# Attention ahead of two expert layers: the first query block's keys in one chunk, a batch's logit products ahead of its transposes, and the value products of two block pairs in one run

## The chip, the cores and the metric

The kernel runs on one core of a Trainium2 chip. The number that counts is the device time of one execution in microseconds (us): 776.23 us is the median of three runs of the kernel before, 775.80 to 778.62. Five engines work side by side, each through its own instructions in the order of the program: TensorE (PE, matrix products and transposes), VectorE (DVE), ScalarE (ACT), GpSimd (POOL) and SyncE (SP, which here issues most of the DMA transfers). They wait for each other through semaphores. PE writes into PSUM, which is cut into eight banks; ACT and DVE copy from there into SBUF.

## The reference, cut to what matters

Three layers follow each other: attention over 4 batches of 8 heads, 768 positions and 64 channels per head, with a local window of 96 keys and 8 global keys, and then two layers of 8 experts over the 3072 tokens. The change is in the attention alone, and in the products with the gates that are interleaved with it:

```python
scores = scale * np.matmul(q, k.transpose(0, 1, 3, 2))
keep = is_global | is_local          # 8 first keys, and the 96 latest up to the query
scores = np.where(keep, scores + bias, -1000000000.0)
scores = scores - np.max(scores, axis=-1, keepdims=True)
a = np.exp(scores)
a = a / (np.sum(a, axis=-1, keepdims=True) + 1e-09)
out = np.matmul(a, v)
...
skip_score = x @ w_skip              # x: the 8 heads' outputs side by side, 512 wide
logits = xc @ w_gate                 # first expert layer
logits = x @ w_gate                  # second expert layer
```

## The kernel before, in words

**Tiling.** A head pair (two heads of one batch, 16 pairs in all) is worked on in six query blocks i of 128 positions. Block 0 sees its own 128 keys. Each other block sees `KW` = 232 keys: 96 before it, its own 128 and the 8 global ones. For the value products the keys stand on partitions, so 232 keys are cut into two chunks r of 116 (keys two by two, even and odd), and block 0's 128 keys, in the same way, into two of 64. `VW` holds the values of blocks 1 to 5, `V0` those of block 0; `load_v` fetches both.

**Units.** Two query blocks (x = 0, 1) of a head pair are a unit, numbered g; there are 48, and j = 0, 1, 2 is a unit's place in its head pair. Block 0 is x = 0 of the unit with j = 0. The stages of a unit are:

- `qk_t`: PE transposes the raw q and k of two blocks into a PSUM tile `pP`, DVE copies the k half into `KT`, POOL copies the keys that the next blocks share, ACT copies the q half into `QT`;
- `s_stage`: PE makes the scores (`pS`, two banks, one unit's worth), DVE adds the bias and takes the extreme of each row (`sb`, `st`);
- `e_stage`: ACT takes the exponentials (`pb`) and their sums;
- `n_stage`: DVE makes the reciprocals of the sums, POOL multiplies `pb` with them, four instructions;
- `t_stage`: PE transposes `pb` of one block into a `pP` tile, DVE copies it to `pts`;
- `o_stage`: PE multiplies `pts` with the values into the one bank `pO`, ACT copies the result to `XT`.

**The order of the work.** One Python loop over g writes all of it, and each engine keeps this order. In its iteration g stand `e_stage(g+2)`, `o_stage(g-1)`, up to two entries of the list `todo`, `n_stage(g+1)`, `t_stage(g)` for both blocks, one part of `qk_t` and `s_stage(g+3)`. I name an iteration by the j of its unit g-1: J0, J1 and J2 follow each other and make up a head pair. On PE an iteration is thus: value products, `todo`, eight transposes of `pb`, four of k and q, four score products (each fp32 product shows as two matmul records in the trace).

**The list `todo`.** When XT has 384 finished positions of a head pair, `x_stage` is put on it (PE transposes them, three in a run, ACT copies to `xs`, SP writes to the tables `xd` and `x2d`). With the last head pair of a batch `logits` (products of XT with the three gates, copied by ACT to `ls`) and `logits_t` (PE transposes `ls`, DVE sums up into `LG`) come behind it. After the last unit what is left of `todo` is worked off, with the steps `ww` (products of the second layer's weights) between, and `route1` sorts the tokens, one batch at a time, on DVE.

**PSUM.** `pP` has five banks that are used in turn by `qk_t`, `t_stage`, `x_stage` and `logits`; `pS` has two, `pO` one.

The lines that write the order of one iteration (before):

```python
        ex(0, 0)
        ex(0, 1)
        if g >= 1:
            o_stage(g - 1)
        if g >= 0:
            one_task()
            if len(todo) > 1:
                one_task()
        if 0 <= g + 1 < NU:
            n_stage(g + 1)
        ex(1, 0)
        if 0 <= g < NU:
            t_stage(g, 0)
            t_stage(g, 1)
        ex(1, 1)
```

Of the kernel before, what the change touches and what calls it, by code (L numbers as in the profile page):

```python
# [7 lines left out]
F32 = mybir.dt.float32  # L8
# [4 lines left out]
AF = mybir.ActivationFunctionType  # L13
# [157 lines left out]
def tile_attn_moe_moe(ctx: ExitStack, tc: tile.TileContext, q, k, v, n_global, n_local,  # L171
                      w_skip, w_gate, w1, w2, w2_gate, w21, w22, out):
    nc = Chip(tc.nc)
    global CK
    CK = ck = nc.clock
    B, H, S, D = q.shape
    G, W = int(n_global), int(n_local)
    HP = H // 2
# [26 lines left out]
    ident = consts.tile([128, 128], F32, name="ident")  # L205
# [42 lines left out]
    ld = att.enter_context(tc.tile_pool(name="ld", bufs=2))  # L248
    wk = att.enter_context(tc.tile_pool(name="wk", bufs=2))
    ps = att.enter_context(tc.tile_pool(name="ps", bufs=1, space=bass.MemoryType.PSUM))  # L250
# [12 lines left out]
    VW, V0 = {}, {}  # L263

    def load_v(b, hp):
        w = VW[b, hp] = ld.tile([KP, NI - 1, 2, 2, D], F32, name="vw", bufs=3)
        z = V0[b, hp] = ld.tile([64, 2, 2, D], F32, name="v0", bufs=3)
        vv = v[b, 2 * hp:2 * hp + 2].rearrange("h (i x) d -> h i x d", x=128)
        nc.sync.dma_start(z.rearrange("p h r d -> p h (r d)"),
                          vv[:, 0].rearrange("h (p r) d -> p h (r d)", r=2))  # L270
        for h in range(2):
            def part(p0, p1, src):
                nc.sync.dma_start(w[p0:p1, :, h].rearrange("p i r d -> p i (r d)"),
                                  src.rearrange("i (p r) d -> p i (r d)", r=2))
            part(W // 2, KP - G // 2, vv[h, 1:])
            part(0, W // 2, vv[h, :NI - 1, 128 - W:])
            part(KP - G // 2, KP, vv[h, 0:1, :G].to_broadcast([NI - 1, G, D]))
# [36 lines left out]
    KT, QT, XT, PB, PT, ST, pO, LS = {}, {}, {}, {}, {}, {}, {}, {}  # L314
# [24 lines left out]


    NG = NI // 2
    GR = [(b, hp, j) for b in range(B) for hp in range(HP) for j in range(NG)]
    SB = {}

    def keys(i):
        return KW if i else 128

    def s_stage(g):
# [11 lines left out]
        for x in range(2):  # L360
            i = 2 * j + x
            SB[g, x] = sb = wk.tile([128, 2, KW], F32, name="sb", bufs=4)
            for h in range(2):
                nc.vector.tensor_tensor_reduce(sb[:, h, :keys(i)], p_s[i, h][:, :keys(i)],
                                               (bias1 if i else bias0)[:, 2 * hp + h, :], 1.0, 3e38,
                                               op0=OP.add, op1=OP.min, accum_out=st[:, 0, x, h:h + 1])

    def e_stage(g, x, h):
        n = keys(2 * GR[g][2] + x)
        if h == 0:  # L370
            PB[g, x] = wk.tile([128, 2, 2, KP], F32, name="pb", bufs=6)
        nc.scalar.activation(PB[g, x][:, h, :, :n // 2].rearrange("p r k -> p k r"),
                             SB[g, x][:, h, :n].rearrange("p (k r) -> p k r", r=2), AF.Exp,
                             bias=ST[g][:, 0, x, h:h + 1], scale=-1.0, accum_out=ST[g][:, 1, x, h:h + 1])
        if h == 1:
            SB.pop((g, x))

    def n_stage(g):
        st = ST.pop(g)
        nc.vector.tensor_scalar(st[:, 2], st[:, 1], 1e-9, None, op0=OP.add)  # L380
        nc.vector.reciprocal(st[:, 2], st[:, 2])
        for x in range(2):
            n = keys(2 * GR[g][2] + x)
            for h in range(2):
                p = PB[g, x][:, h, :, :n // 2]
                nc.gpsimd.tensor_scalar(p, p, st[:, 2, x, h:h + 1], 1.0, op0=OP.mult, op1=OP.mult)

    def t_stage(g, x):
        n = keys(2 * GR[g][2] + x) // 2
        pt = ps.tile([128, 2, 2, 128], F32, name="pP", bufs=5)  # L390
        p = PB.pop((g, x))
        for h in range(2):
            for r in range(2):
                nc.tensor.transpose(pt[:n, h, r, :], p[:, h, r, :n], ident)
        PT[g, x] = wk.tile([128, 2, 2, 128], F32, name="pts", bufs=3)
        nc.vector.tensor_copy(PT[g, x][:n], pt[:n])

    def o_stage(g):
        b, hp, j = GR[g]
        po = ps.tile([128, 2, 128], F32, name="pO")  # L400
        for x in range(2):
            i = 2 * j + x
            n = keys(i) // 2
            t = PT.pop((g, x))
            for r in range(2):
                for h in (1, 0):
                    vv = VW[b, hp][:, i - 1, h, r, :] if i else V0[b, hp][:, h, r, :]
                    nc.tensor.matmul(po[h * 64:(h + 1) * 64, x, :], vv, t[:n, h, r, :], start=r == 0, stop=r == 1)
        if b not in XT:
            XT[b] = wk.tile([128, HP, S], F32, name="xT")  # L410
        nc.scalar.activation(XT[b][:, hp, j * 256:(j + 1) * 256], po.rearrange("p a b -> p (a b)"), AF.Copy)

    def x_stage(b, hp, g):
        px = ps.tile([128, 3, 128], F32, name="pP", bufs=5)
# [407 lines left out]
    todo = [(late_consts, ())]  # L822
# [35 lines left out]
    for g in range(-3, NU + 1):  # L858
        ex = (lambda x, h: e_stage(g + 2, x, h)) if 0 <= g + 2 < NU else lambda x, h: None
        ex(0, 0)  # L860
        ex(0, 1)
        if g >= 1:
            o_stage(g - 1)
        if g >= 0:
            one_task()
            if len(todo) > 1:
# [8 lines left out]
        m, t = divmod(g + 4, NG)  # L875
# [10 lines left out]
        b, hp, j = GR[g - 1]  # L886
        for i in (2 * j, 2 * j + 1):
            beside(b, hp, i)
        if j:
            todo.append((x_stage, (b, hp, j - 1)))  # L890
            if hp == HP - 1:
                todo.append((logits, (b, j - 1)))
                todo.append((logits_t, (b, j - 1)))
                if j == NG - 1:
                    todo.append((start_r1, (b,)))
# [1170 lines left out]
```

## Time and profile before

| what | value |
|---|---|
| median of three runs | 776.23 us (775.80 to 778.62) |
| the profiled execution, its own time | 777.47 us |
| its span, first to last instruction | 775.7 us |
| instructions | 17432 |
| PE, DVE, ACT, POOL busy, share of the span | 96%, 68%, 52%, 60% |
| mean granted TensorE clock | 0.997 of full speed |
| value products of attention, first and last start | 18.5 and 205.8 us |

The page gives busy time by engine over the whole span; the attention is its first 27%. There the engines are far closer to each other than in the means: between 18.5 and 206 us PE is busy for 178 of 187.5 us, DVE for 165 and ACT for 147. A busy PE is a pipeline of matmuls, so the time between the starts of two groups of matmuls says more than the busy time of either.

### The profile page before, as it was taken

What the parts mean: (1) busy time and instruction counts of PE and PEld (TensorE: products, weight loads), DVE (VectorE), ACT (ScalarE), POOL (GpSimd) and SP (SyncE); (2) the same over time, 40 slices, a digit from 0 to 9 for tenths busy, and PEclk for the clock granted to TensorE, in tenths of its full rate; (3) what the DMA queues carried; (4) which work ended last, traced back from release to release, by engine and by line L of the source; (5) the groups of instructions that cost most, each with busy time, mean ns of one, the idle gap of its engine ahead of it and who ended that gap; (6) DMA issues with size and microseconds to landing.
All of it is one profiled execution on the core that took longest, in us unless ns stands there. A gap on an engine that the chain in (4) does not pass through costs nothing.

```text
span 775.7 us, 17432 instructions
## 1 busy us (share of the span) xinstructions
PE 744.8 (96%) x5910; PEld 628.7 (81%) x5910; DVE 526.1 (68%) x1952; ACT 403.3 (52%) x936; POOL 468.2 (60%) x821
## 2 busy tenths in 40 slices
PE   7999999899889999999999999999999999999997
PEld 5887777677659999999888677878788878788986
DVE  5987988979556676777634586778787778752110
ACT  5887787887547655555652113434333434255221
POOL 4664456755214464555793636975768777689911
PEclk9999999999999999999999999999999999999999
DMA  8686988897716766777760035626262636366311
GB/s 192 167 213 167 248 232 200 222 231 199 236 27 213 265 198 195 252 234 224 210 220 33 19 91 191 209 91 222 77 204 84 230 108 206 125 195 185 121 41 41
DMA packets 145370, 132.23 MB, mean 170 GB/s; under 512 B 65427, under 2 KB 112787, under 8 KB 145280
## 3 DMA queue, kind: packets, MB, share of 16 engines
q1 hardware_dynamic: 136896, 111.19, 48.9%
q0 software_dynamic: 6784, 19.51, 7.4%
q8 instruction: 48, 0.79, 0.4%
q10 hardware_dynamic: 1600, 0.39, 0.2%
q14 instruction: 42, 0.34, 0.1%
HBM read 108.80 MB, written 22.79 MB: 170 GB/s over the span
## 4 chain that ended last, share of the span: by engine, by line
PE 44%; POOL 8%; issue 6%; DMA 5%; DVE 4%; ACT 3%; POOLq 0%; DVEq 0%; ACTq 0%; SPq 0%
PE py L132 19%; PE ph L132 19%; POOL wl L132 7%; DMA wr<-in_moe_w_dram 4%; PE pr L132 3%; PE pt L132 3%; ACT wh L132 2%; DVE wl L132 1%; POOL out_dram L132 1%; DMA xg<-x2d,ids 1%; DVE py L132 1%; ACT ya L132 0%; DVE h L132 0%; POOL xg L132 0%; DVE o L132 0%
## 5 line engine op out<-in xcount | busy, mean ns | idle before, releaser
L132 POOL TENSOR_TENSOR wl<-wr,wh 128x256 fp32r<-128x256 f32 x356 | 253.6, 745 | 62.0 <-ACT wh L132 61.3
L132 ACT ACTIVATE wh<-wr 128x1024 fp32r<-128x1024 f32 (+1 forms) x148 | 142.2, 985 | 42.8 <-DMA wr<-in_moe_w_dram 26.8
L132 PE MATMUL py<-wh,h 128*128 128x512 f32 (+1 forms) x448 | 155.9, 401 | 0.0
L132 ACT ACTIVATE h<-ph 128x208 fp32r<-128x208 f32 (+2 forms) x132 | 54.4, 415 | 180.7 <-PE ph L132 168.3
L132 POOL TENSOR_SCALAR pb<-pb,st 128x232 f32<-128x232 f32 (+1 forms) x192 | 83.4, 453 | 74.3 <-ACT pb L132 24.2
L132 ACT ACTIVATE pb<-sb,st 128x232 f32<-128x232 f32 (+1 forms) x192 | 113.8, 664 | 10.1 <-DVE st L132 9.8
L132 DVE SCALAR_TENSOR_TENSOR h<-ph,h 128x208 fp32r<-128x208 f32 (+1 forms) x128 | 58.8, 460 | 88.8 <-ACT h L132 88.7
L132 PE MATMUL ph<-xh,wh 128*128 128x208 f32 (+1 forms) x512 | 99.1, 310 | 1.4 <-DVE h L132 1.4
L132 PE MATMUL ph<-xh,wl 128*128 128x208 f32 (+1 forms) x512 | 100.0, 311 | 0.0
L132 PE MATMUL ph<-xl,wh 128*128 128x208 f32 (+1 forms) x512 | 99.0, 311 | 0.0
L132 PEld LDWEIGHTS py<-wh,h 128*128 128x128 f32 (+1 forms) x448 | 82.0, 185 | 14.1
L132 PE MATMUL py<-wl,h 128*128 128x512 f32 (+1 forms) x224 | 90.9, 406 | 0.0
L132 PEld LDWEIGHTS ph<-xh,wh 128*128 128x128 f32 x512 | 82.2, 190 | 6.8 <-DVE h L132 1.6
L132 PEld LDWEIGHTS ph<-xl,wh 128*128 128x128 f32 x512 | 78.9, 190 | 1.1 <-issue 1.0
L132 PEld LDWEIGHTS ph<-xh,wl 128*128 128x128 f32 x512 | 78.9, 190 | 0.5 <-issue 0.3
L132 DVE TENSOR_TENSOR wl<-wr,wh 128x1024 fp32r<-128x1024 f32 x47 | 61.0, 1304 | 15.3 <-ACT wh L132 15.2
L132 DVE CUSTOM_DVE_ANT_0 sb<-pS,bias 128x232 f32<-128x232 f32 (+1 forms) x192 | 61.4, 374 | 8.9 <-PE pS L132 7.6
L132 DVE COPY pts<-pP 116x512 f32<-116x512 f32 (+1 forms) x96 | 60.7, 672 | 7.6 <-PE pP L132 7.1
L132 POOL DMA_INDIRECT xg<-x2d,ids x24 | 23.8, 990 | 52.2 <-DVE ids L132 19.1
L132 PE MATMUL pS<-kt,qt 64*128 64x232 f32 (+1 forms) x384 | 50.7, 382 | 1.0 <-ACT pb L132 1.0
L132 PE MATMUL pP<-ident,pb 128*116 128x128 f32 (+1 forms) x384 | 51.3, 277 | 0.0
L132 PE MATMUL pO<-pts,vw 116*64 116x128 f32 x640 | 46.3, 281 | 4.0 <-DVE pts L132 3.2
(465 smaller groups left out, 1267.5 us busy)
## 6 DMA issues: line engine op xcount, KB each, us to landing
wr<-in_moe_w_dram SPq DMA_DIRECT2D x136, 512.0 KB
xd<-xs SPq DMA_DIRECT2D x32, 192.0 KB
x2d<-xs SPq DMA_DIRECT2D x32, 192.0 KB
kraw<-in_k_dram SPq DMA_DIRECT2D x30, 192.0 KB
qraw<-in_q_dram SPq DMA_DIRECT2D x30, 192.0 KB
vw<-in_v_dram SPq DMA_DIRECT2D x32, 160.0 KB
vw<-in_v_dram SPq DMA_DIRECT2D x32, 120.0 KB
xT<-in_moe_w_dram SPq DMA_DIRECT2D x1, 1536.0 KB
```

The lines of the kernel that those rows point to most:

```text
L132: r = f(*a, **k)
```

## The change

Four things are done.

1. Block 0's 128 keys are one chunk: its exponentials and its normalised probabilities lie in key order (`probs`), it takes one transpose per head where it took two, its `pts` tile has one r, its copy 256 columns where it had 512, and its value products are two where they were four. `V0` has 128 partitions with 256 bytes per head and partition where it had 64 with 512.
2. `o_stage` takes a list of units. In J0 it isn't called; in J1 it does units j = 0 and j = 1 (four query blocks) into one bank, and ACT copies 512 columns at once; in J2 it does j = 2 as before.
3. `pts` has four buffers where it had three, and the tile's r and h change places.
4. In the last head pair of a batch `logits` goes on `todo` ahead of `x_stage`, not behind it.

```diff
@@ load_v
-        z = V0[b, hp] = ld.tile([64, 2, 2, D], F32, name="v0", bufs=3)
+        z = V0[b, hp] = ld.tile([128, 2, D], F32, name="v0", bufs=3)
         vv = v[b, 2 * hp:2 * hp + 2].rearrange("h (i x) d -> h i x d", x=128)
-        nc.sync.dma_start(z.rearrange("p h r d -> p h (r d)"),
-                          vv[:, 0].rearrange("h (p r) d -> p h (r d)", r=2))
+        nc.sync.dma_start(z, vv[:, 0].rearrange("h p d -> p h d"))
...
+    PTS = 4
...
+    def probs(g, x, h):
+
+        n = keys(2 * GR[g][2] + x)
+        p = PB[g, x][:, h]
+        return p.rearrange("p r k -> p (r k)")[:, :n] if n == 128 else p[:, :, :n // 2]
...
-        nc.scalar.activation(PB[g, x][:, h, :, :n // 2].rearrange("p r k -> p k r"),
-                             SB[g, x][:, h, :n].rearrange("p (k r) -> p k r", r=2), AF.Exp,
+        whole = n == 128
+        o_, i_ = probs(g, x, h), SB[g, x][:, h, :n]
+        nc.scalar.activation(o_ if whole else o_.rearrange("p r k -> p k r"),
+                             i_ if whole else i_.rearrange("p (k r) -> p k r", r=2), AF.Exp,
...
     def t_stage(g, x):
-        n = keys(2 * GR[g][2] + x) // 2
+        n = keys(2 * GR[g][2] + x)
+        nr = 1 if n == 128 else 2
+        n //= nr
         pt = ps.tile([128, 2, 2, 128], F32, name="pP", bufs=5)
-        p = PB.pop((g, x))
         for h in range(2):
-            for r in range(2):
-                nc.tensor.transpose(pt[:n, h, r, :], p[:, h, r, :n], ident)
-        PT[g, x] = wk.tile([128, 2, 2, 128], F32, name="pts", bufs=3)
-        nc.vector.tensor_copy(PT[g, x][:n], pt[:n])
-
-    def o_stage(g):
-        b, hp, j = GR[g]
-        po = ps.tile([128, 2, 128], F32, name="pO")
-        for x in range(2):
-            i = 2 * j + x
-            n = keys(i) // 2
+            p = probs(g, x, h)
+            for r in range(nr):
+                nc.tensor.transpose(pt[:n, r, h, :], p if nr == 1 else p[:, r], ident)
+        PB.pop((g, x))
+        PT[g, x] = wk.tile([128, 2, 2, 128], F32, name="pts", bufs=PTS)
+        nc.vector.tensor_copy(PT[g, x][:n, :nr], pt[:n, :nr])
+
+    def o_stage(gs):
+        b, hp, j0 = GR[gs[0]]
+        po = ps.tile([128, 2 * len(gs), 128], F32, name="pO")
+        for g, x in ((g, x) for g in gs for x in range(2)):
+            i = 2 * GR[g][2] + x
+            y = i - 2 * j0
+            n = keys(i)
+            nr = 1 if n == 128 else 2
             t = PT.pop((g, x))
-            for r in range(2):
+            for r in range(nr):
                 for h in (1, 0):
-                    vv = VW[b, hp][:, i - 1, h, r, :] if i else V0[b, hp][:, h, r, :]
-                    nc.tensor.matmul(po[h * 64:(h + 1) * 64, x, :], vv, t[:n, h, r, :], start=r == 0, stop=r == 1)
+                    vv = VW[b, hp][:, i - 1, h, r, :] if i else V0[b, hp][:, h, :]
+                    nc.tensor.matmul(po[h * 64:(h + 1) * 64, y, :], vv, t[:n // nr, r, h, :],
+                                     start=r == 0, stop=r == nr - 1)
...
-        nc.scalar.activation(XT[b][:, hp, j * 256:(j + 1) * 256], po.rearrange("p a b -> p (a b)"), AF.Copy)
+        nc.scalar.activation(XT[b][:, hp, j0 * 256:(j0 + len(gs)) * 256], po.rearrange("p a b -> p (a b)"), AF.Copy)
...
-        if g >= 1:
-            o_stage(g - 1)
+        if g >= 1 and GR[g - 1][2]:
+            o_stage(range(g - 2 if GR[g - 1][2] == 1 else g - 1, g))
...
         if j:
+            if hp == HP - 1:
+                todo.append((logits, (b, j - 1)))
             todo.append((x_stage, (b, hp, j - 1)))
             if hp == HP - 1:
-                todo.append((logits, (b, j - 1)))
                 todo.append((logits_t, (b, j - 1)))
```

What this does to PE's order around the first unit with j = 0: the rows run from the scores at the end of one iteration through J0 to the start of J1's transposes (`v_126` is the first head pair's `V0`; one row is so many products, each of which is two matmul records in the trace).

```order
 L132 MATMUL pS<-kt,qt 128x128 x2
-L132 MATMUL pO<-pts,v_126 64x128 x4
-L132 MATMUL pO<-pts,vw 64x128 x4
 L132 MATMUL pP<-ident,pb 116x128 x8
 L132 MATMUL pP<-ident,kraw 128x128 x2
 L132 MATMUL pP<-ident,qraw 128x128 x2
 L132 MATMUL pS<-kt,qt 128x232 x4
-L132 MATMUL pO<-pts,vw 64x128 x8
+L132 MATMUL pO<-pts,v_126 64x128 x2
+L132 MATMUL pO<-pts,vw 64x128 x12
 L132 MATMUL pP<-ident,pb 116x128 x8
```

In J0 nothing of `pO` is left ahead of the transposes, and the run in J1 grows from 8 products to 14. In J2 the transposes of block 0 are two where they were four:

```order
 L132 MATMUL pO<-pts,vw 64x128 x8
 L132 MATMUL pP<-ident,xT 128x128 x3
-L132 MATMUL pP<-ident,pb 64x128 x4
+L132 MATMUL pP<-ident,pb 128x128 x2
 L132 MATMUL pP<-ident,pb 116x128 x4
 L132 MATMUL pP<-ident,kraw 128x128 x2
```

At the end of a batch, PE before had in J1 the second logits' products (`xT,wc`) and straight behind them the transposes of their copy (`ls`):

```order
L132 MATMUL pO<-pts,vw 64x128 x8
L132 MATMUL pP<-xT,wc 32x384 x4
L132 MATMUL pP<-ident,ls 128x128 x3
L132 MATMUL pP<-ident,pb 116x128 x8
L132 MATMUL pP<-ident,kraw 128x128 x2
```

With the change the same products stand in J0, an iteration ahead of the transposes of their copy in J1:

```order
L132 MATMUL pP<-ident,ls 128x128 x3
L132 MATMUL pP<-xT,wc 32x384 x4
L132 MATMUL pP<-ident,pb 116x128 x8
L132 MATMUL pP<-ident,kraw 128x128 x2
L132 MATMUL pP<-ident,qraw 128x128 x2
L132 MATMUL pS<-kt,qt 128x232 x4
L132 MATMUL pO<-pts,v_823 64x128 x2
L132 MATMUL pO<-pts,vw 64x128 x12
L132 MATMUL pP<-ident,xT 128x128 x3
L132 MATMUL pP<-ident,ls 128x128 x3
L132 MATMUL pP<-ident,pb 116x128 x8
```

So the second logits' products stand one iteration earlier, and between them and the transposes lie a whole J0 and the long run of value products. Behind the attention, in the two expert layers, no engine's order changes.

## Rows read from the trace of the kernel before

**Rows 1.** Busy time of each engine in stretches (us from the start)

```profile
18.50:206.00 187.50, 178.23 (x1832) 142.91 (x1830) 165.24 (x714) 147.41 (x506) 110.57 (x290) 1.00 0.80 208
20.00:30.00 10.00, 10.00 (x106) 8.27 (x106) 9.90 (x42) 8.85 (x31) 6.60 (x19) 1.00 0.59 149
40.00:60.00 20.00, 20.00 (x214) 16.36 (x210) 17.48 (x75) 17.08 (x59) 12.07 (x34) 1.00 0.80 206
80.00:100.00 20.00, 18.86 (x196) 15.64 (x194) 19.76 (x95) 15.26 (x54) 10.68 (x32) 1.00 0.90 233
100.00:110.00 10.00, 10.00 (x108) 7.47 (x106) 8.06 (x37) 8.68 (x33) 5.72 (x17) 1.00 0.99 258
130.00:150.00 20.00, 16.87 (x172) 13.88 (x169) 19.76 (x91) 15.75 (x56) 14.43 (x35) 1.00 0.86 216
150.00:160.00 10.00, 10.00 (x107) 8.04 (x105) 9.13 (x37) 9.49 (x35) 8.48 (x22) 1.00 0.94 237
180.00:190.00 10.00, 9.40 (x103) 7.88 (x102) 9.83 (x55) 7.53 (x27) 5.35 (x16) 1.00 0.87 242
```

The columns are: stretch and its length, busy time (and instructions) of PE, PE's weight loads, DVE, ACT and POOL, granted clock, DMA share, GB/s.

**Rows 2.** Timeline of PE, one head pair: start, length, group of instructions

```profile
40.23 0.66 PE L132 MATMUL pO<-pts,v 64*64 64x128 f32 x8
...
46.66 1.05 PE L132 MATMUL pS<-kt,qt 64*128 64x232 f32 x8
47.64 1.09 PE L132 MATMUL pO<-pts,vw 116*64 116x128 f32 x16
48.66 0.55 PE L132 MATMUL pP<-ident,xT 128*128 128x128 f32 x3
49.05 1.04 PE L132 MATMUL pP<-ident,pb 128*64 128x128 f32 x8
49.92 0.38 PE L132 MATMUL pP<-ident,kraw 128*128 128x128 f32 x2
50.14 0.38 PE L132 MATMUL pP<-ident,qraw 128*128 128x128 f32 x2
...
51.27 0.66 PE L132 MATMUL pO<-pts,v 64*64 64x128 f32 x8
51.85 0.66 PE L132 MATMUL pO<-pts,vw 116*64 116x128 f32 x8
52.44 0.55 PE L132 MATMUL pP<-ident,xT 128*128 128x128 f32 x3
52.82 1.04 PE L132 MATMUL pP<-ident,pb 128*116 128x128 f32 x8
```

**Rows 3.** Waits on PE from 18.5 to 206 us: total, times, longest

```profile
PE pO L132 <- DVE pts L132: 3.2, 7, 1.0
...
PE pP L132 <- ACT ls L132: 2.2, 3, 0.8
```

**Rows 4.** Timeline of PE where it transposes `ls`, second and last batch

```profile
119.03 0.55 PE L132 MATMUL pP<-ident,ls 128*128 128x128 f32 x3 [0.82 <-ACT ls L132]
...
207.96 0.55 PE L132 MATMUL pP<-ident,ls 128*128 128x128 f32 x3 [0.61 <-ACT ls L132]
```

**Rows 5.** Tiles `pP` and `pO`: copies, count, shortest/median/longest ns

```profile
L132 DVE COPY pts<-pP x96: 651/674/693, 17.3 to 204.7; 116x512 f32<-116x512 f32 x80, 64x512 f32<-64x512 f32 x16
L132 DVE COPY kt<-pP x48: 393/412/424, 4.9 to 192.9; 128x256 f32<-128x256 f32 x48
L132 ACT ACTIVATE w2t<-pP x16: 578/597/607, 209.0 to 227.9; 128x512 f32<-128x512 f32 x16
L132 ACT ACTIVATE xT<-pO x48: 356/364/386, 20.8 to 206.1; 128x256 f32<-128x256 f32 x48
```

**Rows 6.** Timeline of POOL: the four multiplications of `pb` in J2

```profile
49.70 1.75 POOL L132 TENSOR_SCALAR pb<-pb,st 128x232 f32<-128x232 f32 x4 [1.54 <-PE pP L132]
```

**Rows 7.** Timeline of DVE: the last bias operation on the scores that J2 made

```profile
52.22 0.39 DVE L132 CUSTOM_DVE_ANT_0 sb<-pS,bias 128x232 f32<-128x232 f32 x1
```

**Rows 8.** DMA issues: the loads of `V0`, their count and size

```profile
v<-in_v_dram SPq DMA_DIRECT2D x16, 64.0 KB
```

More of the change, by code (lines that the diff above doesn't have):

```diff
@@ L382, in n_stage @@
         for x in range(2):
-            n = keys(2 * GR[g][2] + x)
             for h in range(2):
-                p = PB[g, x][:, h, :, :n // 2]
+                p = probs(g, x, h)
                 nc.gpsimd.tensor_scalar(p, p, st[:, 2, x, h:h + 1], 1.0, op0=OP.mult, op1=OP.mult)
     def t_stage(g, x):
-        n = keys(2 * GR[g][2] + x) // 2
+        n = keys(2 * GR[g][2] + x)
+        nr = 1 if n == 128 else 2
+        n //= nr
         pt = ps.tile([128, 2, 2, 128], F32, name="pP", bufs=5)
-        p = PB.pop((g, x))
@@ L392, in t_stage @@
         for h in range(2):
-            for r in range(2):
-                nc.tensor.transpose(pt[:n, h, r, :], p[:, h, r, :n], ident)
-        PT[g, x] = wk.tile([128, 2, 2, 128], F32, name="pts", bufs=3)
-        nc.vector.tensor_copy(PT[g, x][:n], pt[:n])
-    def o_stage(g):
-        b, hp, j = GR[g]
-        po = ps.tile([128, 2, 128], F32, name="pO")
-        for x in range(2):
-            i = 2 * j + x
-            n = keys(i) // 2
+            p = probs(g, x, h)
+            for r in range(nr):
+                nc.tensor.transpose(pt[:n, r, h, :], p if nr == 1 else p[:, r], ident)
```

## The prediction

> **What bounds the kernel now.** I read the busy time by stretches first, to see which engine the attention runs on. Over its 187.5 us PE is busy for 178, DVE for 165 and ACT for 147, and in a plain stretch (40 to 60 us) PE is busy for all 20 us [rows 1]. So PE's own row of work is the bound, with DVE close behind: DVE has 17.5 of 20 us there and ACT 17.1. Six stretches of 10 us are different: in 20 to 30, 80 to 100, 130 to 150 and 180 to 190 us, 60 us together, DVE is busy for 98 to 99% of the time [rows 1]. There the bias tables are made or the routing of a batch is interleaved, and DVE is as much the bound as PE.
>
> Then the timeline of PE, for what one head pair takes. From one product run with `V0` to the next it is 51.27 - 40.23 = 11.04 us [rows 2], without a wait in it. Last the waits on PE, which are few: 3.2 us for `pts` and 2.2 us for the copy `ls` of the logits, three times, one for each of the first three batches [rows 3]; a fourth such wait, 0.61 us, stands behind the last unit at 207.96 [rows 4]. All that comes after the attention waits for its last tokens, so I take what is saved there as saved in the total.
>
> **The change part by part.**
>
> *Transposes of block 0.* Eight transposes of `pb` take 49.92 - 49.05 = 0.87 us from start to start, 0.109 each, and two of k, which are 128 by 128, take 0.22, 0.11 each [rows 2]. Four of 64 keys become two of 128: 4 x 0.109 - 2 x 0.11 = 0.22 us saved a pair. The width hardly shows in these rows, so I give no bounds but 0.18 to 0.22.
>
> *Value products of block 0.* Eight matmul records with 64 keys take 51.85 - 51.27 = 0.58 us, eight with 116 keys 52.44 - 51.85 = 0.59 [rows 2]: the number of keys costs nothing. So four records with 128 keys should take half, 0.29 saved. The form with 128 rows isn't in the trace. Bounds: 0, if a record with 128 keys took twice as long, and 0.32; I take 0.29, since 64 and 116 keys cost the same.
>
> *One run for four blocks.* Eight records on their own take 0.59, sixteen in one run 48.66 - 47.64 = 1.02, or 0.51 for eight [rows 2]. A run so costs some 0.08 us to begin, and one run a pair goes away. Bounds 0 and 0.15 (both halves of J0 against half of J1's). Sum of the three: 0.22 + 0.29 + 0.08 = 0.59 a pair, **9.4 us** over 16 pairs; by the bounds 2.9 to 11.
>
> *Logits first.* The three waits for `ls`, 2.2 us, go, because an iteration now lies between the copy and its transposes. Of the 0.61 behind the last unit a run of three transposes, 52.82 - 52.44 = 0.38 [rows 2], covers all but 0.2. **2.6 us**, bounds 1.5 (new waits in place of some) and 2.9. The writes of `xs` that SP issues move behind by one entry; nothing reads them before the gathers after the attention.
>
> *Copies.* DVE's copy for block 0 shrinks to the shape of the `kt` copy: 0.674 to 0.412, 0.26 us a pair. ACT's two copies of 256 columns become one of 512, for which `w2t` is the row: 2 x 0.364 - 0.597 = 0.13 us a pair [rows 5]. Neither is on the path in plain stretches; there DVE falls from 17.48 / 20 x 11.04 = 9.65 to 9.4 us a pair and ACT from 9.43 to 9.3, both below the 10.45 us that PE would take.
>
> *Given back where DVE is the bound.* In the 60 us from above, 5.4 pairs, time can fall only as far as DVE's work does, 0.26 and not 0.59: 0.33 x 5.4 = **1.8 us lost**. Bounds: 0, as some of PE's waits there lie ahead of J0's products, which now come later and would find their `pts` ready, and 3.2, if nothing is won there.
>
> *Cover that goes.* In J0 the value products, 52.44 - 51.27 = 1.17 us [rows 2], stood between the scores and the next transposes. What they covered is the chain by which the transposes in J0 get their input: scores in J1 start at 46.66, DVE's bias, reciprocals, then POOL's four multiplications until 49.70 + 1.75 = 51.45 [rows 6], 4.79 us after; for the first block, two of the four, 3.92. With the change PE goes from those scores to those transposes in 0.98 (scores) + 3.63 (J2, 47.64 to 51.27) - 0.22 (block 0's transposes) + 0.38 (`x_stage`) = 4.77 us, and to the second block's 0.43 later, 5.20 [rows 2]. So 0.85 us of slack are left for the first block and 0.41 for the second, where there were 2.2 and 1.8. Nothing waits by these numbers. Behind a transpose that waits stand, on PE, k and q of a coming pair and the scores, and for these DVE and ACT wait. As 0.41 is little and the copies that feed it jitter by some 0.1, I put 0.1 us a pair, **1.6 us lost**; bounds 0 and 0.41 x 16 = 6.6. In J1 the long run, 0.29 + 3 x 0.51 = 1.8 us, reads the `pts` of j = 0 first, so that DVE has until its second half for those of j = 1. The scores in J0 need the banks that DVE reads in its bias operations; they come 0.38 + 0.87 + 0.44 = 1.7 us after J0's start, and DVE is through 52.22 + 0.39 - 51.27 = 1.34 us after it [rows 7]. The fourth `pts` buffer is what keeps both units' tiles.
>
> *V0's load.* 16 loads of 64 KB [rows 8], in pieces of 256 bytes where they were 512. At 206 GB/s for a DMA share of 0.80 [rows 1] 64 KB take 0.25 us of all DMA engines. If the smaller pieces cost double, the share in a plain stretch goes from 0.80 x 11.04 = 8.8 us a pair to 9.1 of 10.45, 0.87: still covered, and the loads are issued two pairs ahead. The Trainium skill ("DMA: Bandwidth & Descriptors", section Specifications) says that transfers below 512 bytes miss line rate because of a read-modify-write, which speaks against this edit and for the rival on DMA below. No row here shows what it costs: q and k come in rows of 64 floats, 256 bytes, already, and PE waits for none of them in the plain stretch. By the rule, read as a doubling, the 0.25 us would be paid wherever DMA is the bound; without it, nothing.
>
> **Sum.** 9.4 + 2.6 - 1.8 - 1.6 = 8.6 us. The profiled execution takes 777.47 us, 1.77 more than its span and 1.24 more than the median, and would take 768.9; the median goes from 776.23 to **767.6**. A measurement of this kernel tells 0.5%, 3.9 us, from no change; so under 772.35 is faster and over 780.1 slower.
>
> **The rivals.**
>
> *The short J0 is paid back as a wait.* J0 has 1.17 us less on PE, and DVE and ACT have as much to do in it as before. If they can't use the slack of J1, PE stands still in J0 for about what the pair saves, 0.59, and only the logits are won: 776.2 - 2.6 = 773.6, within 0.5%. For it: DVE and ACT are at 87 and 85% even in plain stretches, and `pS` holds one unit's worth, so PE can't run ahead. Against it: the slacks above.
>
> *The chain to POOL is longer than its cover (slower).* The same place, with one price: all of the 1.17 us comes back as a wait for POOL's `pb` in every J0, since the transposes stand right behind the scores. 16 x (1.17 - 0.59) - 2.6 = 6.7 us more: 783. It decides from a wait of 0.59 + 2.6 / 16 = 0.75 us a pair, that is when the chain takes 5.2 + 0.75 = 5.95 us where it takes 4.79. For it: nothing else stands between in J0 but `x_stage`. Against it: POOL has 12.1 of 20 us to do [rows 1] and starts as soon as DVE's reciprocals are there.
>
> *DMA becomes the bound.* In 100 to 110 and 150 to 160 us the DMA share is 0.99 and 0.94 [rows 1], since weights for the expert layers are fetched beside. There nothing can be won, and `V0`'s pieces cost their 0.25: two pairs lose 2 x (0.59 + 0.25) = 1.7 us, and if the neighbouring stretches at 0.86 to 0.90 follow in part, some 3: 770.6.
>
> *It isn't carried to the end.* The last loads for the products `ww` and the first gather could set the start of the first expert layer, and half of the saving would be lost: 772. Against it: PE has no wait for a load there.
>
> **How the numbers follow.** Forecast 0.66, with a range of its own of 764 (the logits' upper bound, nothing lost in DVE's stretches, a larger saving by the runs) to 771; paid back in J0 0.13; DMA 0.07; not carried 0.05; slower 0.09. The range 764 to 774.5 takes in all but the slower case and the edges, and the lower bounds of single terms. Faster: 0.66 + 0.07 + 0.03 of the case at 772 = 0.76; within 0.5%: 0.13 + 0.02 = 0.15; slower 0.09.
>
> **What the profile after would show.** A head pair in a plain stretch takes 10.4 to 10.6 us where it takes 11.04; four `v` records in a run of 28 take about 1.8 us; no wait for `ls` on PE between 18.5 and 206 us; DVE's copy of block 0 takes 0.41. The rivals would show as waits of 0.5 us and more ahead of J0's transposes (for `pb`) or scores (for `sb`), as a DMA share of 1.0 with PE waiting for `kraw` or `qraw`, or as attention ending 8 us earlier and the total not. The forecast is wrong if the records with 128 keys take longer than those with 116, or if DVE's in-order queue makes the even J1 and J0 unequal in a way that I haven't followed.

## The result, and the profile after

The changed kernel takes 768.75 us (median of 4 runs, 766.83 to 770.46), the kernel before on the same chip 776.54 (775.80 to 778.62). The ratio is 0.9889, with a 95% interval of 0.9866 to 0.9912: 1.1% faster, 8.6 us by the ratio; the medians themselves lie 7.8 us apart. The profiled execution takes 770.19 us with a span of 768.4.

First the busy time of the changed kernel by stretches, with the columns of [rows 1]; three of the stretches are new, two in the attention and one in the expert layers:

```profile
18.50:206.00 187.50, 181.02 (x1839) 141.33 (x1838) 163.55 (x724) 150.94 (x504) 109.05 (x289) 1.00 0.84 219
20.00:30.00 10.00, 10.00 (x108) 8.44 (x105) 9.89 (x42) 8.62 (x31) 6.77 (x18) 1.00 0.73 186
40.00:60.00 20.00, 20.00 (x214) 16.26 (x213) 17.27 (x72) 18.07 (x61) 12.41 (x35) 1.00 0.84 214
...
70.60:82.40 11.80, 11.42 (x115) 9.12 (x114) 11.35 (x64) 8.94 (x33) 6.13 (x18) 1.00 0.82 197
...
129.00:142.50 13.50, 11.82 (x109) 8.62 (x108) 13.33 (x56) 10.76 (x38) 10.12 (x24) 1.00 0.89 237
...
463.30:470.20 6.90, 6.90 (x63) 5.26 (x62) 2.62 (x9) 0.00 (x0) 4.04 (x6) 0.51 0.64 212
```

PE is still busy for all of the plain stretch, 40 to 60 us, and DVE is no nearer to the bound there than before (17.27 of 20). From 129 to 142.5 us it is the other way round: DVE 13.33 of 13.5, PE 11.82. The last line is one to come back to: a granted clock of 0.51, which is the lower of the two levels (1.2 GHz) nearly throughout, in a place that had 1.00 before.

Then the timeline of PE in the changed kernel: the scores of the second head pair, one plain head pair (41.29 to 51.59), the first gathered transposes behind the attention, and a stretch of the first expert layer:

```profile
16.65 0.88 PE L132 MATMUL pS<-kt,qt 64*128 64x232 f32 x8
...
41.29 0.44 PE L132 MATMUL pO<-pts,v 128*64 128x128 f32 x4
...
46.82 0.82 PE L132 MATMUL pP<-ident,pb 128*128 128x128 f32 x6
47.47 0.38 PE L132 MATMUL pP<-ident,kraw 128*128 128x128 f32 x2
...
48.00 0.88 PE L132 MATMUL pS<-kt,qt 64*128 64x232 f32 x8
...
49.20 1.04 PE L132 MATMUL pP<-ident,pb 128*116 128x128 f32 x8
...
51.59 0.44 PE L132 MATMUL pO<-pts,v 128*64 128x128 f32 x4
51.85 1.48 PE L132 MATMUL pO<-pts,vw 116*64 116x128 f32 x24
53.27 1.09 PE L132 MATMUL pP<-ident,pb 128*116 128x128 f32 x8
...
222.31 0.94 PE L132 MATMUL py<-ident,xg 128*128 128x128 f32 x8 [2.12 <-issue]
...
454.98 0.76 PE L132 MATMUL pr<-oh,gm 128*32 128x8 bf16 x24
...
459.40 0.50 PE L132 MATMUL py<-wh,h 128*128 128x512 f32 x1 [0.72 <-ACT h L132]
461.01 0.76 PE L132 MATMUL pr<-oh,gm 128*32 128x8 bf16 x24 [1.11 <-DVE gm L132]
...
472.39 0.31 PE L132 MATMUL pr<-oh,gm 128*16 128x32 bf16 x6
```

The same places in the kernel before, outside [rows 2]:

```profile
17.68 0.88 PE L132 MATMUL pS<-kt,qt 64*128 64x232 f32 x8
...
232.39 1.65 PE L132 MATMUL py<-ident,xg 128*128 128x128 f32 x8 [2.21 <-issue]
...
466.82 0.76 PE L132 MATMUL pr<-oh,gm 128*32 128x8 bf16 x24
...
480.14 0.31 PE L132 MATMUL pr<-oh,gm 128*16 128x32 bf16 x6
```

The reader is to see three things. A plain pair takes 51.59 - 41.29 = 10.30 us where it took 11.04 [rows 2]. From the scores of the second pair to the first gathered transposes it is 222.31 - 16.65 = 205.66 us where it was 232.39 - 17.68 = 214.71: 9.05 us won, and I use this distance for the attention in every kernel below, because the start-up ahead of it moves by 1.5 us from one execution to the next. And the lead isn't kept: at 454.98 it is 466.82 - 454.98 = 11.84 us, at 472.39 it is 480.14 - 472.39 = 7.75. Between these places the changed kernel takes 17.41 us and the kernel before 13.32.

Not all of the 11.84 us is the attention's: 9.05 are, 17.68 - 16.65 = 1.03 is the earlier start, and the other 1.76 came behind the first gathered transposes. Part of that is a lower clock that only the kernel before had there (the changed kernel has 1.00 from 222 to 236 us):

```profile
232.00:236.00 4.00, 3.61 (x21) 3.18 (x21) 1.60 (x3) 2.46 (x4) 1.18 (x2) 0.57 0.39 110
```

What is late between 454.98 and 472.39 us is a load of expert weights, as ACT's timeline of the changed kernel shows:

```profile
457.91 1.06 ACT L132 ACTIVATE wh<-wr 128x1024 fp32r<-128x1024 f32 x1 [5.23 <-DMA wr<-in_moe_w_dram]
458.87 0.85 ACT L132 ACTIVATE h<-ph 128x384 fp32r<-128x384 f32 x2
```

In the kernel before ACT waits 3.60 us at this load. Behind its copy stands ACT's `h`, for which PE waits at 459.40.

The waits on PE in the changed kernel, from 18.5 to 198 us (total, times, longest), against [rows 3]:

```profile
PE pO L132 <- ACT xT L132: 1.6, 4, 0.8
PE pS L132 <- issue: 1.3, 1, 1.3
PE pP L132 <- POOL pb L132: 1.1, 2, 0.7
PE pO L132 <- ACT pb L132: 1.0, 1, 1.0
PE pO L132 <- DVE pts L132: 0.9, 3, 0.4
```

No wait for `ls` is left. The wait for POOL, which the slower rival was about, exists, but twice only and for 1.1 us (three times and for 1.5 and 1.4 us in the two repeats below). POOL's rows of this chain, once beside the making of bias tables on DVE and once in the plain stretch:

```profile
37.23 2.12 POOL L132 TENSOR_SCALAR pb<-pb,st 128x232 f32<-128x232 f32 x4 [1.72 <-ACT pb L132]
...
47.47 1.75 POOL L132 TENSOR_SCALAR pb<-pb,st 128x232 f32<-128x232 f32 x4 [1.73 <-ACT pb L132]
```

In the plain stretch POOL is done at 47.47 + 1.75 = 49.22, its first two of four at 48.35; the transposes start at 49.20 and reach the second block at 49.63. That leaves 0.85 and 0.41 us, the two slacks that the prediction worked out from the rows of before.

The 1.3 us under `issue` come by way of a transfer. `xs` has two buffers; ACT's copy into one of them waits until an earlier transfer to `x2d` has read it, and behind this copy stands ACT's copy to `QT`, which PE's next scores need (ACT's rows, then PE's, in the last head pair):

```profile
183.94 0.49 ACT L132 ACTIVATE xs<-pP 128x384 f32<-128x384 f32 x1 [3.79 <-DMA x2d<-xs]
...
185.42 0.37 ACT L132 ACTIVATE qt<-pP 128x256 f32<-128x256 f32 x1
...
185.89 1.05 PE L132 MATMUL pS<-kt,qt 64*128 64x232 f32 x8 [1.26 <-issue]
```

ACT waits for such a transfer in each of the ten profiles of this document that have logits ahead of `x_stage`, 0.6 to 9.0 us in the attention, and in neither of the two that have them behind. In the repeats of the change below PE loses nothing by it; in this execution it lost 1.26 us. Why the transfer is late isn't shown.

### The profile page after: what moved, and what is told of

Its sections match the earlier page's. It is cut to its first block, busy times and chain, and to the rows that moved or that the text cites. A ratio compares the mean times of both kernels' runs of the same rounds, so it can differ in the third digit from the quotient of the medians.

```text
span 768.4 us, 17196 instructions
## 1 busy us (share of the span) xinstructions
PE 739.3 (96%) x5814; PEld 621.5 (81%) x5814; DVE 523.8 (68%) x1952; ACT 400.7 (52%) x920; POOL 466.6 (61%) x821
## 4 chain that ended last, share of the span: by engine, by line
PE 43%; POOL 12%; issue 8%; DMA 3%; DVE 3%; ACT 2%; POOLq 0%; DVEq 0%; ACTq 0%; SPq 0%
PE py L132 19%; PE ph L132 18%; POOL wl L132 10%; PE pr L132 3%; DMA wr<-in_moe_w_dram 3%; PE pt L132 2%; POOL out_dram L132 1%; ACT wh L132 1%; DMA xg<-x2d,ids 1%; POOL xg L132 1%; DVE wl L132 1%; DVE py L132 0%; ACT ya L132 0%; DVE o L132 0%; DVE gm L132 0%
## 5 line engine op out<-in xcount | busy, mean ns | idle before, releaser
L132 ACT ACTIVATE pb<-sb,st 128x232 f32<-128x232 f32 (+1 forms) x192 | 112.1, 646 | 7.4 <-DVE st L132 6.3
L132 DVE COPY pts<-pP 116x512 f32<-116x512 f32 (+1 forms) x96 | 57.2, 632 | 4.7 <-PE pP L132 4.2
L132 PEld LDWEIGHTS pP<-ident,pb 128*116 128x116 f32 (+1 forms) x352 | 38.6, 137 | 11.1 <-POOL pb L132 6.2
```

The lines of the kernel that those rows point to most:

```text
L132: r = f(*a, **k)
```

## The experiments

In all of them the distance named above is the attention; ratios are to the kernel before on the same chip. The lengths of fourteen head pairs, each from the start of its first unit's scores to that of the next pair's (differences of starts on PE's timeline, as 16.65 and 48.00 above), in us:

| pair | 2 | 3 | 4 | 5 | 6 | 7 | 8 | 9 | 10 | 11 | 12 | 13 | 14 | 15 |
|---|---|---|---|---|---|---|---|---|---|---|---|---|---|---|
| before | 10.71 | 11.03 | 11.03 | 11.94 | 12.87 | 11.50 | 12.55 | 11.94 | 13.01 | 12.16 | 13.98 | 11.94 | 12.92 | 11.50 |
| logits first alone | 10.93 | 11.03 | 11.03 | 11.82 | 12.26 | 11.76 | 12.31 | 11.81 | 12.26 | 12.19 | 13.72 | 11.82 | 12.26 | 11.69 |
| change without the run | 10.56 | 10.45 | 10.45 | 11.23 | 11.71 | 11.76 | 11.84 | 11.23 | 11.72 | 12.11 | 13.52 | 11.23 | 11.71 | 11.57 |
| the change | 10.75 | 10.30 | 10.30 | 11.08 | 11.56 | 11.76 | 11.84 | 11.08 | 11.56 | 12.12 | 13.54 | 11.42 | 11.56 | 11.57 |
| the change again | 11.48 | 10.30 | 10.30 | 11.08 | 11.56 | 11.76 | 11.85 | 11.08 | 11.56 | 12.12 | 13.52 | 11.42 | 11.56 | 11.58 |
| POOL 1 us later | 12.20 | 11.15 | 11.15 | 11.52 | 11.56 | 12.21 | 12.56 | 11.63 | 11.55 | 12.61 | 14.34 | 12.11 | 11.56 | 11.93 |

Beside pairs 7, 8, 11, 12 and 15 the routing of a batch runs.

**The change again.** No edit.

> The changed kernel once more. In its first profile the first transposes of gathered tokens (the end of the attention's chain) start at 222.31 us where the kernel before has 232.39, 10.1 us earlier, but the span is only 7.3 us shorter: between 459 and 470 us PE waits 1.8 us for a weight load, the granted clock falls to half, and some 4 us are given back. Theory: that is how four loads in flight happened to land, and no work of the change. Then this profile has the same 222.3 within 0.3 us, and where the wait at that place is short and the clock stays, the span is about 765 us and the time 766.5 to 767.5. Rival: the earlier end of the attention brings it about, and it stands in every execution: 770 us again, with the clock at half near 465 us.

Measured: 773.09 us (767.86 to 776.24) against 779.41 on this chip, ratio 0.9888 (0.9843 to 0.9933). The attention takes 221.62 - 16.39 = 205.23 us, 9.5 less than before. Against the first profile pair 2 is 0.73 us longer, since PE waits 0.41 and 0.37 us for POOL in it, and what lies behind pair 15 is 1.16 us shorter (44.06 for 45.22), since the late transfer of `xs` doesn't hold PE up. So a difference of half a microsecond between two kernels is within what one program shows from one execution to the next. The late weight load and a lower clock behind it came again, so this one execution didn't tell whether they belong to the change; the runs below do.

**Logits first alone**, on the kernel before:

```diff
+            if hp == HP - 1:
+                todo.append((logits, (b, j - 1)))
             todo.append((x_stage, (b, hp, j - 1)))
             if hp == HP - 1:
-                todo.append((logits, (b, j - 1)))
                 todo.append((logits_t, (b, j - 1)))
```

> The kernel before with nothing but the logits' products put ahead of the transposes. Theory (PE's row is the bound, each wait taken from it is won): the three waits for ls go, the attention's chain ends 2.2 to 2.8 us earlier (first gathered transposes at 229.6 to 230.2 us), time 773.5 to 774.5. Rival: the products in J0 and the transposes in J1 meet other waits (the pP banks, the copy of XT), and under 1 us is won: 231.5 us or later.

Measured: 776.32 us (775.58 to 778.97), ratio 0.9964 (0.9948 to 0.9979). PE's timeline of this kernel:

```profile
16.89 0.88 PE L132 MATMUL pS<-kt,qt 64*128 64x232 f32 x8
...
229.06 0.93 PE L132 MATMUL py<-ident,xg 128*128 128x128 f32 x8 [2.21 <-issue]
```

212.17 us, 2.5 less than before. The table shows where: in pairs 6, 10 and 14, some 0.7 each, while pairs 7 and 15 get 0.3 and 0.2 longer.

**One chunk alone**, with three `pts` buffers, a product run for each pair of blocks, and logits behind:

```diff
-    PTS = 4
+    PTS = 3
...
-        if g >= 1 and GR[g - 1][2]:
-            o_stage(range(g - 2 if GR[g - 1][2] == 1 else g - 1, g))
+        if g >= 1:
+            o_stage(range(g - 1, g))
...
-            if hp == HP - 1:
-                todo.append((logits, (b, j - 1)))
             todo.append((x_stage, (b, hp, j - 1)))
             if hp == HP - 1:
+                todo.append((logits, (b, j - 1)))
```

> The kernel before with block 0's keys in one chunk and nothing else (separate runs of value products, logits behind, three pts buffers). Theory: 0.22 us of transposes and 0.32 of products a pair, 0.54, all of it won in plain pairs (11.04 becomes 10.50) and about half in the six pairs where routing work makes DVE the bound: 16 x 0.54 - 6 x 0.28 = 7.0 us, first gathered transposes at 225.4 us, time near 769.5. Rival (the long run and the later place of J0's products are what wins): under 5 us, 227.4 us or later.

Measured: 772.50 us (771.28 to 773.20), ratio 0.9906 (0.9877 to 0.9934). PE's timeline of this kernel:

```profile
17.77 0.88 PE L132 MATMUL pS<-kt,qt 64*128 64x232 f32 x8
...
39.46 0.44 PE L132 MATMUL pO<-pts,v 128*64 128x128 f32 x4
...
49.91 0.44 PE L132 MATMUL pO<-pts,v 128*64 128x128 f32 x4
...
226.03 0.94 PE L132 MATMUL py<-ident,xg 128*128 128x128 f32 x8 [2.14 <-issue]
```

A plain pair takes 10.45 us and the attention 208.26, 6.45 less than before. Logits and chunk by themselves give 2.5 + 6.45 = 8.95 of the 9.05 us.

**Without the long run**, all else as changed:

```diff
-        if g >= 1 and GR[g - 1][2]:
-            o_stage(range(g - 2 if GR[g - 1][2] == 1 else g - 1, g))
+        if g >= 1:
+            o_stage(range(g - 1, g))
```

> The changed kernel with the value products of each unit in a run of their own, as before; chunk, four buffers and logits as changed. Theory: the run is worth the 0.19 us a pair that PE's starts show (11.04 to 10.30 a pair in all), so a plain pair takes 10.50 us and the attention's chain ends 16 x 0.19 = 3 us later than in the changed kernel, less what the long run costs as waits in J0 where DVE is late: 2 to 3 us, first gathered transposes at 224.3 to 225.3 us. Rival (the short J0 pays the run back as waits in the routing stretches): no difference, 222.3 us, or earlier.

Measured: 769.39 us (769.11 to 771.72), ratio 0.9871 (0.9838 to 0.9903). PE's timeline of this kernel:

```profile
16.58 0.88 PE L132 MATMUL pS<-kt,qt 64*128 64x232 f32 x8
...
222.36 1.60 PE L132 MATMUL py<-ident,xg 128*128 128x128 f32 x8 [2.21 <-issue]
```

205.78 us, 0.12 more than with the run. My theory of 2 to 3 us fell. By the table the run wins 0.15 in each of seven pairs, 1.06 in all, nothing in the five pairs with routing, and loses 0.19 in pairs 2 and 13; that leaves 0.68 over these pairs. In pair 2 the changed kernel's transposes at 18.89 us wait 0.36 for POOL; without the run no wait for POOL is listed. In the two repeats of the change pair 2 takes 11.48 and 11.44 us, and nothing of the 0.68 is left.

**The change and the change without the run, five rounds each**, to see whether the run moves the total. Edits as above.

> The changed kernel a third time, in five rounds beside the version without the long run (e9). So far the changed kernel's executions spread over 8 us on one chip (767.9 to 776.2) and those of the version without the run over 2.6 us (769.1 to 771.7), though the attention ends at the same time in both. Theory: the spread is stretches in which the granted clock is at half, about 1.7 us lost in each, which fall by chance into the expert layers of either kernel; then with more executions both show the same median within 2 us and the same lowest time within 1 us. Rival: the long run itself brings more of them (or the late first weight load at the second expert layer, seen in four of six profiles of kernels with the run and in none of four without), and the median is 3 us or more above e9's.

> The changed kernel without the long run once more, in five rounds. Theory: median within 2 us of e8's, lowest time within 1 us, attention's chain ending at 222.4 us within 0.7, and in this profile or e8's the first weight load of the second expert layer may take 3.8 us or 5.4 us in either. Rival: median 3 us or more below e8's, spread under 4 us, load at 3.8 us.

Measured: with the run 771.26 us (767.86 to 774.25), ratio 0.9899 (0.9872 to 0.9926); without it 770.30 (768.11 to 770.84), ratio 0.9871 (0.9849 to 0.9893). The attention takes 205.17 and 205.71 us. The intervals overlap and the lowest times are 0.25 us apart, so the run has no effect on the total that these runs can tell; the version without it is, if anything, ahead. So the gain that these runs can tell in the total is that of the chunk and the logits. In this profiled execution with the run the weight load came early. Over all profiles it was late in four of the seven with the run and in none of the four with the change or a part of it but no run, so the run isn't enough to make it late, and whether it makes it likelier stays open.

**Three `pts` buffers** under the changed order:

```diff
-    PTS = 4
+    PTS = 3
```

> The changed kernel with three pts buffers where it has four. Theory (the fourth buffer carries the run): with three, DVE's copy for the second block of j = 1 must wait until PE has read block 0's tile, which it does only in J1, so DVE stands for over 1 us in J0 with the kt copy and the next bias operations behind it. DVE has 9.4 us of work in a pair of 10.3, so a plain pair becomes 10.6 to 11.1 us and the attention's chain (first gathered transposes, 222.3 and 221.6 us in the two profiles of the changed kernel) ends 4 to 10 us later. Rival (DVE makes it up in J1): under 1 us.

Measured: 775.46 us (770.48 to 778.85), ratio 0.9941 (0.9918 to 0.9964), the attention 225.02 - 17.89 = 207.13. I had expected more, 4 to 10 us. DVE's timeline in a pair beside the bias tables:

```profile
43.08 0.66 DVE L132 COPY pts<-pP 116x512 f32<-116x512 f32 x1
...
44.38 0.69 DVE L132 COPY pts<-pP 116x512 f32<-116x512 f32 x1 [0.65 <-PE pO L132]
```

The second copy has no buffer until PE's run has read one: the engines are locked in step. Pairs 3 and 4 take 11.00 us for 10.30, most of the others 0.14 more, and those with routing, but for one with 0.23, nothing. So without the fourth buffer the long run costs more than it wins. The ratio is 0.005 above that of the change, 4 us, of which the attention shows 1.5; the rest isn't shown, but four of the eight executions have a mean granted clock of 0.990 to 0.992, and the three shortest one of 0.997 or 0.998.

**Block 0's values loaded twice**, the second copy unread, so that the small pieces and their bytes are doubled:

```diff
-        nc.sync.dma_start(z, vv[:, 0].rearrange("h p d -> p h d"))
+        z2 = ld.tile([128, 2, D], F32, name="v0b", bufs=1)
+        for u in (z2, z):
+            nc.sync.dma_start(u, vv[:, 0].rearrange("h p d -> p h d"))
```

> The changed kernel with block 0's values loaded twice, the second copy unread: 64 KB more in pieces of 256 bytes a pair. Theory (DMA is covered by loads that are issued two pairs ahead, also at shares of 0.99): no wait of PE for k, q or v, the attention's chain ends at 222.3 us within 0.7, DMA share in 40 to 60 us up from 0.84 to 0.86 or 0.88. Rival (the smaller pieces cost where DMA is at its limit): 0.25 us or more in each pair of the stretches at 0.9 and above, 224 us or later.

Measured: 776.27 us (770.22 to 781.28, 10 runs), ratio 0.9959 (0.9929 to 0.9989); the attention 224.30 - 17.37 = 206.93, 1.3 more than changed, where my theory allowed 0.7. The busy time of this kernel in a stretch where DMA was nearly full before, and in the twelfth pair:

```profile
100.00:110.00 10.00, 10.00 (x100) 7.31 (x98) 7.71 (x34) 8.53 (x30) 4.76 (x14) 1.00 0.97 240
129.84:144.32 14.48, 11.84 (x110) 8.65 (x109) 13.28 (x57) 10.43 (x38) 9.46 (x24) 1.00 1.00 257
```

In the first PE is busy throughout, at a DMA share of 0.97, and the pairs here take 11.08 and 11.56 us as in the changed kernel; plain pairs take 10.30. The twelfth pair is longer, 14.48 for 13.54, at a DMA share of 1.00 where the changed kernel has 0.89. ACT waits there for a buffer of `xs`, as in the last pair of the changed kernel, and PE's scores are late behind it:

```profile
137.63 0.49 ACT L132 ACTIVATE xs<-pP 128x384 f32<-128x384 f32 x1 [3.82 <-DMA x2d<-xs]
...
139.59 1.05 PE L132 MATMUL pS<-kt,qt 64*128 64x232 f32 x8 [0.85 <-issue]
```

So the loads of q, k and v don't bound the attention, with twice the load of block 0 either, but DMA isn't without a price: ACT waits for writes of `xs` in three places, 9.0 us in all, against 3.8 in one place of the changed kernel's first profile and 2.2 and 1.2 in the repeats. In the total the ratio is 0.007 above that of the change, 5 us. Where the rest goes the one profiled execution (772.0) doesn't show; the ten executions run from 770.22 us at a mean granted clock of 0.998 to 781.28 at 0.988, so part of the spread goes with the clock. The Trainium skill ("DMA: Bandwidth & Descriptors", section Specifications) would have the pieces below 512 bytes miss line rate. No run here shows that rule by itself: this one doubles pieces and bytes together, and its 0.94 us in the twelfth pair can be due to either.

**POOL later by one or by two operations.** An idle multiplication on an unused tile, 0.46 us, or two, 1.01 us, stands ahead of POOL's multiplications of the unit with j = 1, the chain whose cover the change shortens:

```diff
+    idle = ac.tile([128, KW], F32, name="idle")
+    nc.gpsimd.memset(idle, 0.0)
...
+        if GR[g][2] == 1:
+            for _ in range(1):
+                nc.gpsimd.tensor_scalar(idle, idle, st[:, 2, 0, 0:1], 1.0, op0=OP.mult, op1=OP.mult)
         for x in range(2):
```

> The changed kernel with one idle POOL multiplication of 128 by 232, about 0.45 us, ahead of the four that feed the transposes in J0. By the profile of the changed kernel POOL ends these at 49.22 us where PE begins its eight transposes at 49.20, so the second block's input has about 0.4 us of slack and the first one's 0.85. Theory: the 0.45 us use the slack up and hardly more: 0 to 0.15 us a pair, the attention's chain ends at 222 to 224.5 us. Rival (J0 has no slack and each delay of the chain is paid): 0.45 x 16 = 7 us, 229 us.

> The same with two idle multiplications, about 0.9 us. Theory: 0.4 us of slack go, 0.5 us are paid a pair in the plain pairs and less where the run in J1 or DVE's routing work covers: 4 to 8 us, the attention's chain ends at 226 to 230 us, and PE shows a wait for pb ahead of the second block's transposes in J0. Rival (the slack is larger than the rows say, since PE makes the wait up in J1): no difference from one idle multiplication, 222 to 224.5 us.

Measured: with one 773.47 us (772.32 to 774.52), ratio 0.9922 (0.9898 to 0.9945), the attention 225.41 - 17.70 = 207.71, 2.05 more than changed or 0.13 a pair; with two 779.32 (776.20 to 784.85), ratio 1.0010 (0.9983 to 1.0036), the attention 231.33 - 17.82 = 213.51. POOL's timeline with one, beside the bias tables:

```profile
39.26 0.46 POOL L132 TENSOR_SCALAR idle<-idle,st 128x232 f32<-128x232 f32 x1 [1.69 <-DVE st L132]
```

PE's timeline with two, in a pair beside the bias tables and in a plain one:

```profile
42.96 1.30 PE L132 MATMUL pP<-ident,pb 128*116 128x128 f32 x6 [0.21 <-POOL pb L132]
...
53.52 1.47 PE L132 MATMUL pP<-ident,pb 128*116 128x128 f32 x8
```

Eight transposes take 1.47 us in the plain pair, 0.43 more than the 1.04 of the changed kernel, and the wait ahead of 42.96 has its group of six stretched too (1.30, where six took 0.82). With one idle operation pairs 3 and 4 take 10.59 and 10.60, 0.30 more than 10.30, and pair 5 is unchanged at 11.08; with two it is 0.85 and 0.44 more. So the slack is 0.46 - 0.30 or 1.01 - 0.85 = 0.16 us beside the bias tables, and 1.01 - 0.44 = 0.57 in pair 5, where one operation cost nothing. Two operations use up 213.51 - 205.66 = 7.9 of the 9.05 us.

## Why the prediction was right, point by point

The forecast of 767.6 us, 8.6 less, holds: 768.75, and 8.6 us less by the ratio. But the sum came out so closely because terms that were off went against each other.

*Transposes of block 0*: right. Six now take 47.47 - 46.82 = 0.65 us for 0.87, 0.22 saved.

*Value products of block 0*: right. Four records with 128 keys take 51.85 - 51.59 = 0.26 us for 0.58; 0.32 saved, the upper bound, where 0.29 was taken.

*One run*: mis-sized in both ways. The other 24 products take 53.27 - 51.85 = 1.42 us, which is 0.19 less than the 0.59 + 1.02 of before, above the bound of 0.15. Counted per pair it is worth 0.15 (10.45 to 10.30), but not sixteen times: 0.68 us over fourteen pairs in the first profile and nothing in the two repeats, where the prediction had 0.08 x 16 = 1.3.

Together a plain pair saves 0.73 us, not 0.59: for sixteen pairs 11.7 instead of 9.4.

*Logits first*: right in size, 2.5 us where 2.6 was forecast; the wait is gone from the list. What the prediction put at nothing is the later writes of `xs`: it asked only who reads the tables, and not that ACT's next copies need the buffers. In the first profile that cost PE 1.26 us in the last pair.

*Given back where DVE is the bound*: the mechanism was right, its size and one of its places were not. Between logits first alone and the whole change, the five pairs with routing save 0, 0.47, 0.07, 0.18 and 0.12 us, 0.84 of 5 x 0.73 = 3.65: 2.8 us lost where 1.8 was forecast. They take the same time with the run and without it, and DVE is at 13.33 of 13.5 us in one of them and at 11.35 of 11.8 in another. That DVE sets the length of such a pair in the changed kernel shows in pair 7, here with logits first alone and with one chunk alone:

```profile
70.52:82.29 11.77, 11.77 (x123) 9.78 (x122) 11.20 (x56) 8.51 (x30) 6.65 (x21) 1.00 0.88 224
...
69.56:80.70 11.14, 11.07 (x113) 9.21 (x114) 10.50 (x55) 7.33 (x26) 6.22 (x19) 1.00 0.82 208
```

From the first of these to the changed kernel (70.60 to 82.40 us) PE has 8 instructions less, but DVE 64 for 56 and as much to do, 11.35 us for 11.20, and the pair keeps its length. With one chunk alone PE has about as many as changed, 113 for 115, but DVE only 10.50 us, and the pair takes 11.14 us. So with PE's work taken out the pair keeps its length, and with DVE's taken out it doesn't. How much of DVE's other work falls into a pair differs between the kernels (55 to 64 instructions here), which the prediction didn't count. What wasn't so is 20 to 30 us, where DVE shows 9.89 of 10 as before and the pairs win all of their 0.73: DVE's busy share alone didn't tell a bound from an engine that has just enough to do.

*Cover that goes*: right that it costs something, but 1.6 us was put down as 0.1 in each pair, and plain pairs wait for nothing. It is paid in pairs 2 and 13, which fall short of the 0.73 by 0.9 us together in the first profile and by 1.6 in the repeats; without the run no wait for POOL is listed. The slack in the plain stretch was worked out as 0.41 and showed itself between 0.46 and 0.57. Beside the bias tables it is only 0.16, because POOL's four multiplications take 2.12 us there.

*V0's load*: no wait of PE for it, as forecast. Doubling it left the pairs from 100 to 110 us as they were, and cost 0.94 us in the one pair where the DMA share came to 1.00.

So for chunk and run the forecast was 9.4 - 1.8 - 1.6 = 6.0 us. The fourteen pairs show 14 x 0.73 = 10.2, less 2.8 in the routing pairs and 1.0 in pairs 2 and 13 and the rounding of the others: 6.45 in the first profile, and some 5.7 in the repeats, where pair 2 is longer. With 2.5 for the logits it is 9.0 in the attention. In the repeats the whole attention comes to 9.5, as the last pair has no late transfer. That the parts meet the 8.6 is in part luck: a plain pair saves more than forecast and the routing pairs lose more.

*Carried to the end*: mostly. In the profiled execution 11.84 - 7.75 = 4.1 us of the lead go between 454.98 and 472.39 us: PE waits 0.72 and 1.11 us (0.48 in the kernel before), both for what stands behind the late weight load (ACT's `h` behind its copy of the load, DVE's `gm` behind its part of `h`), and from 463.3 to 470.2 the granted clock is 0.51. The kernel with one idle POOL operation parts the two, as its load is late and its clock isn't low (1.00 from 465 to 477 us). ACT's row, then PE's:

```profile
464.86 1.06 ACT L132 ACTIVATE wh<-wr 128x1024 fp32r<-128x1024 f32 x1 [4.97 <-DMA wr<-in_moe_w_dram]
...
462.19 0.76 PE L132 MATMUL pr<-oh,gm 128*32 128x8 bf16 x24
...
476.87 0.31 PE L132 MATMUL pr<-oh,gm 128*16 128x32 bf16 x6
```

It takes 476.87 - 462.19 = 14.68 us for the stretch. The eight profiles with an early load take 13.09 to 13.32, and the three with a late load and a low clock 16.39, 16.41 and 17.41. So the late load costs 1.4 to 1.6 us and the low clock 1.7 to 2.7 more. The rival that the lead isn't carried to the end was right for this execution, though by a mechanism I hadn't in mind. It isn't a fixed price of the change: with the same program it is absent in the profiled execution of the repeat over five rounds, which takes 769.84 us on a chip where the kernel before takes 779.82 and not 776.54.

Of the rivals, the short J0 isn't paid back in plain pairs. The slower one is a true mechanism, decided by less than was said: a chain later by 1.01 us costs 7.9 us in the attention and all of the gain in the total (ratio 1.0010), where 0.41 of slack + 0.75 of wait = 1.16 us had been named.

## What to carry to other kernels

On the engine that bounds a stretch, count the records: here two transposes or four matmul records of a product less were worth 0.11 and 0.08 us each, with 64, 116 or 128 keys. Before the work is taken out from between a producer and its reader, work out the cover in us from both ends of the chain, in the stretch where the producer is slowest and not in a plain one. And a saving is won only in the pairs where that engine ends last: to know which these are, look for pairs that don't move when PE's work is changed, since a full DVE alone doesn't show it, and compare the other engine's work in the same pair. Where a stage is moved, ask also which buffers its neighbours' transfers hold, and for how long.

## What I had not expected of the hardware

A late weight load in the expert layers comes with 1.6 to 1.8 us of waits on PE in four profiles, and in three of them a stretch at a granted clock of 0.50 or 0.51 follows. In the fourth the clock stays at 1.00, so the late load by itself doesn't bring it. Such stretches also come at other places: at 232 us in the kernel before (0.57), at 397 in the first repeat of the change (0.50). They come in some executions and not in others of the same program, and kernels with the change spread over more (767.86 to 776.24 in the first repeat, where the longest has a mean granted clock of 0.992 and the shortest 0.999). Why the weight load is late in some executions stays open: from its issue to its use by ACT it takes 5.2 to 5.5 us in four profiles and 3.6 to 3.8 in the other eight, and the program of the expert layers is the same in all.

POOL's four multiplications of 128 by 232 take 2.12 us beside DVE's making of the bias tables and 1.75 elsewhere. One of the four is longer: 0.82 us where the others take 0.46, three times in the changed kernel, each time while DVE runs the operation that makes the table (`bias<-rel,msk`).
